# Half of chunk 1's first layer between the parts of chunk 0's second layer, with later joins

## The chip, the cores and the metric

One core of a Trainium2 chip runs the whole kernel. The metric is the device time of one execution in microseconds. Executions of one kernel agree within about 0.3%, and what is argued about here is 0.1% to 0.5%, so every comparison below is of several fast executions of a kernel with those of the kernel before on the same chip, with a 95% interval. Engines: TensorE (PE), its weight loads (PEld), VectorE (DVE), ScalarE (ACT), GpSimd (POOL) and SyncE (SP). The granted clock is the share of TensorE's full clock that its throttle lets through, as the trace records it.

## The reference

```python
def _attn_ref(q, k, v, beta):           # 4 x 8 heads, 768 tokens, head size 48
    k_n = k / (norm(k) + 1e-06)
    for t in range(S):
        y[t] = q[t] @ state
        v_old = state.T @ k_n[t]
        state = state + beta[t] * outer(k_n[t], v[t] - v_old)
def _moe_ref(x, w_in, w_out):           # x is y as 3072 x 384; w_in 384 x 2048
    h = x @ w_in
    return (0.5 * h * (1 + erf(h / sqrt(2)))) @ w_out
```

Inputs and outputs are fp32. What arrives as weights must be decoded on the chip first, on DVE with one step per part on ACT.

## The kernel before

The sequence is cut into 12 chunks of 64 tokens. In each chunk the recurrence becomes small matrix products and a triangular solve. DVE eliminates row by row for two chunks at a time (a group), in blocks of 32. "Joins" then put the blocks together: level 0 (`psJ<-XM,G`) goes back to DVE for a product into XM, level 1 (`psJ<-Zf,XM`) to ACT for a copy into Zf. The chain of a chunk then goes through small products: queries (psG, masked on DVE into P), state products (psK), the solve (psU, copied into U), and from U the output x and the new state (both psY); x is turned (psX) into xT, the feed-forward's input. The feed-forward layer follows: first layer (psH, with a Gelu on ACT), second layer (psO). A scheduler decides the instruction order from a plan of times in which one unit is one chunk's feed-forward. The parts that the change touches (cuts are marked `...`):

```python
def back(x):                       # group g, in eliminate_steps; x = 0, 1, 2
    ...                            # DVE transposes: XM, then twice Zf
    if x == 2:
        for cc in range(2):
            for p in range(2):     # four parts of Zf are cleared
                if g == cc == p == 0: nc.scalar.mul(part, low[...], 0.0)
                else: nc.gpsimd.memset(part, 0.0)

def fc1(c, f):                     # one of 16 first-layer steps
    psH = ps.tile([128, NA * 128], F32, tag="mlp", name="psH")
    for m in range(NM): nc.tensor.matmul(psH, ...)
    nc.scalar.activation(G[:, f, :], psH, ACT.Gelu)

def ffn_steps(c):
    ones = [(1.3, fc1, c, f) for f in range(NF)]
    ...
    twos = [(2.7, fc2, tiles[c, a], f, f + 4) for a in range(NA) for f in range(0, NF, 4)]
    if c == 0: twos.sort(key=lambda s: s[3])
    return ones + twos
...                                # start-up by hand, then the plan
back2[0](*back2[1:])
for a in range(NA): join(0, (a,), 1)
...
plan = [at(c + 1, c + 2, ffn_steps(c)) for c in range(NC)]
plan += [..., at(2.58, 2.74, join_steps(1)), at(2.72, 2.98, state_steps(2)), ...]
```

Of the kernel before, what the change touches and what calls it, by code (L numbers as in the profile page):

```python
# [8 lines left out]
F32 = mybir.dt.float32  # L9
# [7 lines left out]
def kernel(  # L17
# [29 lines left out]
    B, H, S, D = q.shape  # L47
# [235 lines left out]
    def sum_of_squares(u, h):  # L283

        if "both" not in ns:
            n23 = wk.tile([128, 2 * NA, H], F32, tag="n0", name="n0", bufs=1)
            ns[2], ns[3] = n23[:, 0:NA], n23[:, NA:]
            ns["both"] = n23
        if h == 0:
            u.ksq = wk.tile([128, H, D], F32, tag="ksq", name="ksq")  # L290
        nc.scalar.activation(u.ksq[:, h], u.Kn[:, h, 0:D], ACT.Square,
                             accum_out=ns[u.c][:, u.a, h:h + 1])
# [96 lines left out]
    def queries(us):  # L389
        c = us[0].c  # L390
        psP = products(us, 1)
        if c not in Ps:
            Ps[c] = (su if c == 1 else wk).tile([128, NA * H, C], F32, tag=f"P{c == 1}", name="P",
                                                bufs=1)
        for u in us:
            u.P = Ps[c][:, u.a * H:(u.a + 1) * H]
        dst = heads(Ps[c][:, us[0].a * H:(us[-1].a + 1) * H])
        if c < 2:
            nc.scalar.copy(dst, psP)
        else:  # L400
            both = mask.unsqueeze(1).to_broadcast([128, len(us) * H, C])
            nc.vector.tensor_tensor(dst, psP, heads(both), op=ALU.mult)  # L402
# [19 lines left out]
    def eliminate_steps(g):  # L422
        steps = []

        def scales():
            gt = wk.tile([128, HB], F32, tag="gt", name="gt", bufs=1)
            gl = XMs[g] = wk.tile([128, NU, HB], F32, tag="XM", name="XM", bufs=1)
            nc.vector.transpose(gt, gms[g].rearrange("q t h -> q (t h)"))
            nc.gpsimd.tensor_tensor(gl, low, gt.unsqueeze(2).to_broadcast([128, HB, HB]),
                                    op=ALU.mult)  # L430

        def flip():
            Nus[g] = wk.tile([128, HB, HB], F32, tag="Nu", name="Nu", bufs=1)
            nc.vector.transpose(Nus[g], Ds[g].rearrange("q u n -> q n u"))
            nc.vector.tensor_tensor(Nus[g], Nus[g], XMs[g], op=ALU.mult)

        def eliminate(j):
            nu = Nus[g]
            n = HB - 1 - j
            tmp = wk.tile([128, HB * HB // 4], F32, tag="tmp", name="tmp")  # L440
            tmp = tmp[:, 0:n * j].rearrange("q (i c) -> q i c", i=n)
            nc.vector.tensor_tensor(tmp, nu[:, j + 1:, j:j + 1].to_broadcast([128, n, j]),  # L442
                                    nu[:, j:j + 1, 0:j].to_broadcast([128, n, j]), op=ALU.mult)
            nc.vector.tensor_tensor(nu[:, j + 1:, 0:j], nu[:, j + 1:, 0:j], tmp, op=ALU.add)  # L444

        def diagonal():
            flat = Nus[g].rearrange("q i c -> q (i c)")
            nc.vector.memset(flat[:, 0:HB * HB:HB + 1], 1.0)

        def back(x):  # L450
            nu = Nus[g]
            if x == 0:
                nc.vector.transpose(XMs[g].rearrange("q u c -> q c u"),
                                    nu.rearrange("q i c -> q c i"))
            else:
                cols = slice(HB, C) if x == 1 else slice(0, HB)
                nc.vector.transpose(Zf[g % 2][:, :, cols].rearrange("q u i -> q i u"), nu)  # L457
            if x == 2:
                for cc in range(2):
                    for p in range(2):  # L460
                        part = Zf[g % 2][p * C + HB:(p + 1) * C,
                                         cc * NU // 2:(cc + 1) * NU // 2, 0:HB]
                        if g == cc == p == 0:
                            nc.scalar.mul(part, low[0:HB, 0:HB // 2], 0.0)
                        else:
                            nc.gpsimd.memset(part, 0.0)  # L466

        steps = [(0.3, scales), (3.0, flip)]
        steps += [(0.7, eliminate, j) for j in range(1, HB - 1)]
        steps += [(0.1, diagonal)]  # L470
        steps += [(1.9, back, x) for x in range(3)]
        return steps

    def join(g, ts, level, copy=nc.scalar.copy):

# [190 lines left out]


    FH = NF // 2
    DH = DM // 2
    B11, B12 = w_out_sb[:, 0:FH, 0:DH], w_out_sb[:, 0:FH, DH:]  # L670
    B21, B22 = w_out_sb[:, FH:, 0:DH], w_out_sb[:, FH:, DH:]
    T = {}

    def fc1(c, f):
        psH = ps.tile([128, NA * 128], F32, tag="mlp", name="psH")
        for m in range(NM):
            nc.tensor.matmul(psH, lhsT=w_in_sb[:, f // 2, m, f % 2 * 128:(f % 2 + 1) * 128],  # L677
                             rhs=xTs[c][:, m, :], start=(m == 0), stop=(m == NM - 1))
        nc.scalar.activation(G[:, f, :], psH, ACT.Gelu)  # L679
# [112 lines left out]
    def ffn_steps(c):  # L792
        ones = [(1.3, fc1, c, f) for f in range(NF)]
        if c > 1:
            return [(1.3, first_layer, c, f) for f in range(NF)] + [
                (2.6, second_layer, c, n) for n in (1, 5, 2, 6, 4, 7, 3)]
        twos = [(2.7, fc2, tiles[c, a], f, f + 4) for a in range(NA) for f in range(0, NF, 4)]
        if c == 0:
            twos.sort(key=lambda s: s[3])
        return ones + twos  # L800

    def at(first, last, steps):

# [10 lines left out]
    def signs(c0, c1):  # L814
        psB = sq("psB", c1 - c0, B * H)
        for c in range(c0, c1):
            nc.tensor.transpose(psB[:, c - c0, :], bt[:, c].rearrange("n p t -> n (p t)"),
                                ident[0:B * H, 0:B * H])
        for p in range(2):
            src = psB[HALF[p]].rearrange("q c (a p h) -> q c a p h", p=2, h=H)[:, :, :, p, :]  # L820
            nc.scalar.mul(beta_m[HALF[p], c0:c1], src, -1.0)
# [19 lines left out]
    signs(0, 2)  # L841
    diagonals(first[3])
    root(n0)
    scales_, flip_, *rows, back0, back1, back2 = [s_[1:] for s_ in eliminate_steps(0)]
    factors(gms[0], beta_m[:, 0:2].rearrange("q c a h -> q (c a) h"), n0)
    scales_[0]()
    flip_[0]()
# [1 line left out]
    for u in first:  # L849
        grams([u])  # L850
    signs(2, NC)
    for u in first:
        transposed(u, (1,))
        queries([u])
    for a in range(NA):
        fetch_in(tiles[2, a].Qp[:, :, 0:D], q, tiles[2, a])
# [4 lines left out]
    for n in range(n_in, n_in + len(slots)):  # L861
        fetch(n)
    load_v(1)
    third = [tiles[2, a] for a in range(NA)]
    for u in third:
        transposed(u, (0,))
    grams(third)
    for u in third:
        transposed(u, (1,))
# [14 lines left out]
    back2[0](*back2[1:])  # L884
    for a in range(NA):
        join(0, (a,), 1)
    for u in first[NA:]:
        scale_v(u)
    begin(0)
# [27 lines left out]
    def late():  # L917
# [3 lines left out]
        for a in range(NA):  # L921
# [3 lines left out]
            for c in range(5, NC, 2):  # L925
                tiles[c, a].Kb = Kb

    plan = [at(c + 1, c + 2, ffn_steps(c)) for c in range(NC)]
    plan += [at(0.985, 1.26, decode_steps(3, n_in)), at(1.26, 1.65, decode_steps(n_in, NW)), at(1.66, 1.67, [(1.0, late)])]
    plan += [at(0.98, 0.985, [(1.0, load, 3)]),  # L930
             at(1.02, 1.1, [(1.0, join, 0, range(NA, 2 * NA), level) for level in range(2)]),
]
    sums = [(1.0, sum_of_squares, tiles[c, a], h) for c in (2, 3) for a in range(NA) for h in range(H)]
    plan += [at(1.08, 1.5, sums), at(1.51, 1.511, [(1.0, prep, c) for c in (2, 3)]), at(1.65, 1.655, [(1.0, finish_both)]), at(2.97, 2.971, [(1.0, finish, 4)]), at(2.675, 2.676, [(1.0, queries, third)]),
             at(1.12, 1.6, state_steps(1)),
             at(1.75, 2.45, eliminate_steps(1)),
             at(2.58, 2.74, join_steps(1)), at(2.72, 2.98, state_steps(2)),
             at(2.67, 2.671, [(1.0, prep, 4)]), at(2.8, 2.9, [(1.0, grams, [tiles[4, a] for a in range(NA)])])]
    plan += [at(0.995, 1.0, [(1.0, load_v, 2)]), at(2.98, 2.981, [(1.0, sums_of_w)]), at(3.1, 3.11, [(1.0, last_sum_of_w)])]
    plan += [at(c - 0.4, c - 0.3, v_steps(c)) for c in range(4, NC)]  # L940
    plan += [at(2.08, 2.44, [(1.0, scale_head, tiles[c, a], h)
# [2 lines left out]
    for c in range(4, NC):  # L944
        us = [tiles[c, a] for a in range(NA)]
        t = {4: 1.8, 5: 2.1}.get(c, c - 2.9)
        plan += [at(t, t + 0.01, [(1.0, load_blocks, c, "Kb", k)])]
        t = 3.2 if c == 4 else c - (1.3 if c % 2 == 0 else 0.9)
        plan += [at(t, t + 0.01, [(1.0, load_blocks, c, "Qb", q)])]
        t = c - (2.1 if c % 2 == 0 else 2.6) if c > 5 else {4: 2.1, 5: 2.69}[c]  # L950
        plan += [at(t, t + 0.01, [(1.0, load_k, c, "Kn")])]
        plan += [at(c - 0.4, c - 0.39, [(1.0, load_k, c, "Kp")])]
        t = {4: 2.73, 5: 2.95}.get(c, c - (1.97 if c % 2 == 0 else 2.36))
        plan += [at(t, t + 0.01, [(1.0, turned_k, u) for u in us])]
        t = c + (0.05 if c % 2 == 0 else -0.34)
        plan += [at(t, t + 0.01, [(1.0, turned_q, u) for u in us])]
# [56 lines left out]
```

## Time and profile before

| | |
|---|---|
| time | 671.02 us median of 3 runs (670.69 to 671.75) |
| profiled execution | span 670.1 us, a fast one but slower than the three timed (671.82 us of device time) |
| busy | PE 96%, DVE 67%, ACT 34%, POOL 12% |
| start-up, to about 84 us | DVE full, PE 50% to 90% |
| from 178.55 us, chunk 2's first layer | PE without gaps, 101 us per two chunks |

The page's row of the granted TensorE clock (tenths of full speed, 40 slices of 16.75 us):

```profile
PEclk8576999999999999999999999999999999999999
```

The first four slices, the start-up, have less than the full clock. The other lines of before stand in the prediction.

### The profile page before, as it was taken

What the parts mean: (1) busy time and instruction counts of PE and PEld (TensorE: products, weight loads), DVE (VectorE), ACT (ScalarE), POOL (GpSimd) and SP (SyncE); (2) the same over time, 40 slices, a digit from 0 to 9 for tenths busy, and PEclk for the clock granted to TensorE, in tenths of its full rate; (3) what the DMA queues carried; (4) which work ended last, traced back from release to release, by engine and by line L of the source; (5) the groups of instructions that cost most, each with busy time, mean ns of one, the idle gap of its engine ahead of it and who ended that gap; (6) DMA issues with size and microseconds to landing.
All of it is one profiled execution on the core that took longest, in us unless ns stands there. A gap on an engine that the chain in (4) does not pass through costs nothing.

```text
span 670.1 us, 21705 instructions
## 1 busy us (share of the span) xinstructions
PE 640.3 (96%) x9542; PEld 559.4 (83%) x9542; DVE 452.3 (67%) x921; ACT 228.6 (34%) x605; POOL 82.1 (12%) x82
## 2 busy tenths in 40 slices
PE   5767998999999999999999999999999999999997
PEld 4656775866689989989989989989989989989997
DVE  6999999994689846489846479846479844324021
ACT  3357754714342143142143142143142133122220
POOL 4051300103111021111021111021111010000000
PEclk8576999999999999999999999999999999999999
DMA  9785655203431232511332511211401210100101
GB/s 130 174 253 167 121 172 135 48 0 66 81 51 32 53 53 44 82 31 30 55 49 49 84 29 26 53 21 30 68 3 24 55 20 3 24 2 2 24 1 25
DMA packets 158431, 39.76 MB, mean 59 GB/s; under 512 B 150016, under 2 KB 153216, under 8 KB 158336
## 3 DMA queue, kind: packets, MB, share of 16 engines
q1 hardware_dynamic: 152464, 33.40, 26.3%
q10 hardware_dynamic: 5872, 4.97, 3.2%
q8 instruction: 75, 1.23, 0.8%
q14 instruction: 20, 0.16, 0.1%
HBM read 33.62 MB, written 4.72 MB: 57 GB/s over the span
## 4 chain that ended last, share of the span: by engine, by line
PE 82%; DVE 10%; ACT 3%; issue 2%; DMA 2%; SPq 1%; DVEq 0%; ACTq 0%
PE psH L677 36%; PE psX L715 12%; PE psY L715 12%; PE psZ L715 4%; PE psJ L517 3%; PE psK L572 3%; PE psG L367 3%; PE psO L690 2%; PE psU L597 2%; DVE Nu L444 2%; DVE tmp L442 2%; PE psY L615 1%; DVE w_e L235 1%; DVE w_out_sb L236 1%; PE psY L624 1%
## 5 line engine op out<-in xcount | busy, mean ns | idle before, releaser
L677 PE MATMUL psH<-xT,w_in_sb 128*128 128x256 f32 x1152 | 261.5, 383 | 2.3 <-ACT G L679 2.3
L677 PEld LDWEIGHTS psH<-xT,w_in_sb 128*128 128x128 f32 x1152 | 215.6, 190 | 33.7 <-ACT G L679 3.9
L679 ACT ACTIVATE G<-psH 128x256 f32<-128x256 f32 x192 | 73.3, 382 | 180.4 <-PE psH L677 168.3
L444 DVE TENSOR_TENSOR Nu<-Nu,tmp 128x30 f32<-128x30 f32 (+9 forms) x180 | 61.8, 343 | 6.2
L442 DVE TENSOR_TENSOR tmp<-Nu 128x30 f32<-128x30 f32 (+9 forms) x180 | 61.6, 342 | 5.1
L715 PE MATMUL psX<-w_out_sb,G 128*128 128x192 f32 x320 | 56.2, 329 | 0.0
L715 PE MATMUL psY<-w_out_sb,G 128*128 128x192 f32 x304 | 54.1, 329 | 0.6
L715 PEld LDWEIGHTS psX<-w_out_sb,G 128*128 128x128 f32 x320 | 52.2, 190 | 0.7
L715 PEld LDWEIGHTS psY<-w_out_sb,G 128*128 128x128 f32 x304 | 49.1, 190 | 2.1 <-DVE u L761 1.8
L690 PE MATMUL psO<-w_out_sb,G 128*128 128x384 f32 x128 | 45.1, 495 | 1.6 <-DVE w_out_sb L236 1.6
L660 ACT COPY xT<-psX 128x384 f32<-128x384 f32 x24 | 11.3, 476 | 102.9 <-PE psX L659 102.8
L306 POOL TENSOR_TENSOR n<-n,half 128x16 f32<-128x16 f32 x10 | 29.4, 2938 | 87.9 <-DVE n L281 66.9
L690 PEld LDWEIGHTS psO<-w_out_sb,G 128*128 128x128 f32 x128 | 23.1, 190 | 16.9 <-DVE w_out_sb L236 4.0
L603 ACT COPY U<-psU 64x192 f32<-64x192 f32 x96 | 30.0, 313 | 19.5 <-PE psU L597 18.3
L402 DVE TENSOR_TENSOR P<-psG,mask 128x1024 f32<-128x1024 f32 x10 | 12.2, 1224 | 35.6 <-PE psG L367 35.6
L580 DVE TENSOR_TENSOR W<-psK,V 128x384 f32<-128x384 f32 x22 | 12.1, 552 | 29.1 <-ACT y L579 29.0
L466 POOL MEMSET Zf<- 32x512 f32 x23 | 12.4, 541 | 154.5 <-DVE Zf L457 153.6
L724 DVE TENSOR_TENSOR S<-G 128x512 f32<-128x512 f32 x20 | 13.7, 687 | 25.8 <-ACT G L679 25.7
L332 POOL TENSOR_TENSOR V<-V,n 128x384 f32<-128x384 f32 x18 | 17.1, 958 | 106.1 <-DMA V<-in_v_dram 67.6
L638 DVE TENSOR_TENSOR x<-psY,y 64x192 f32<-64x192 f32 x80 | 28.3, 354 | 0.9
L715 PE MATMUL psY<-T,G 128*128 128x192 f32 x160 | 28.2, 329 | 0.0
L715 PE MATMUL psX<-T,G 128*128 128x192 f32 x160 | 28.1, 329 | 0.0
(138 smaller groups left out, 866.9 us busy)
## 6 DMA issues: line engine op xcount, KB each, us to landing
Kp<-in_k_dram SPq DMA_DIRECT2D x76, 96.0 KB, 3.6
w_out_sb<-in_moe_w_in_dram SPq DMA_DIRECT2D x24, 256.0 KB, 4.2
V<-in_v_dram SPq DMA_DIRECT2D x48, 96.0 KB, 2.9
out_dram<-o_sb ACTq DMA_DIRECT2D x46, 96.0 KB, 2.2
w_raw<-in_moe_w_out_dram SPq DMA_DIRECT2D x10, 384.0 KB, 5.4
Zf<-in_moe_w_out_dram SPq DMA_DIRECT2D x6, 384.0 KB, 5.1
Qp<-in_q_dram SPq DMA_DIRECT2D x64, 32.0 KB, 2.2
Qp<-in_q_dram SPq DMA_DIRECT2D x16, 96.0 KB, 4.3
```

What stands on the lines that cost most here:

```text
L306: nc.gpsimd.tensor_tensor(flat, flat, half, op=ALU.pow)
L367: nc.tensor.matmul(psG[HALF[p], r, i * NP + j, :], lhsT=u.Kt[rows, p, j, :], rhs=(u.Qt if x else u.Kt)[rows, p, j, :], start=True, stop=True)
L442: nc.vector.tensor_tensor(tmp, nu[:, j + 1:, j:j + 1].to_broadcast([128, n, j]), nu[:, j:j + 1, 0:j].to_broadcast([128, n, j]), op=ALU.mult)
L444: nc.vector.tensor_tensor(nu[:, j + 1:, 0:j], nu[:, j + 1:, 0:j], tmp, op=ALU.add)
L517: nc.tensor.matmul(psJ[to, i, :], lhsT=(xm if level else off)[rows, u, :], rhs=zf[rows, u, HB:C] if level else xm[rows, u, :], start=True, ...
L572: nc.tensor.matmul(u.psK[to, x, r, j, :], lhsT=(u.Qt if x else u.Kt)[rows, p, j, :], rhs=St[rows, u.a, p, j, :], start=True, stop=True)
L603: copy(pairs(u.U[HALF[p]], s), u.psU[HALF[p ^ s], p])
L638: nc.vector.tensor_tensor(dst, src, pairs(u.y[HALF[p ^ s]], s), op=ALU.add)
L677: nc.tensor.matmul(psH, lhsT=w_in_sb[:, f // 2, m, f % 2 * 128:(f % 2 + 1) * 128], rhs=xTs[c][:, m, :], start=(m == 0), stop=(m == NM - 1))
L679: nc.scalar.activation(G[:, f, :], psH, ACT.Gelu)
L690: nc.tensor.matmul(u.psO, lhsT=G[:, f, u.a * 128:(u.a + 1) * 128], rhs=w_out_sb[:, f, :], start=(f == 0), stop=(f == NF - 1))
L715: nc.tensor.matmul(ps_, lhsT=lhs[:, f, :], rhs=rhs[:, f, :], start=first and f == 0, stop=f == FH - 1, skip_group_check=not first)
```

## The change

The intent is to fill TensorE's waits for decoded output weights in chunk 0's second layer with half of chunk 1's first layer (C), to start the decode earlier by taking a clear out of the way of ACT's copies (A), to move 16 squares of chunk 2's norm into start-up (B), and to place the joins and what follows later in the plan (D). The lines are shortened, those of the plan to the times that change; the tile of the moved sums also gets another buffer.

```diff
-            if x == 2:
+            if x == 2 and g > 0:
+                clear(g)
+        def clear(g):
                 for cc in range(2): ...
-        return steps
+        return steps + [(0.0, clear, 0)] if g == 0 else steps      # A
...
+    EARLY = 8
     def fc1(c, f):
-        psH = ps.tile([128, NA * 128], F32, tag="mlp", name="psH")
+        if c == 1 and f < EARLY: psH = dn("psH")[:, 0, 0:NA * 128]
+        else: psH = ps.tile([128, NA * 128], F32, tag="mlp", name="psH")
...
         if c == 0:
             twos.sort(key=lambda s: s[3])
-        return ones + twos
+            more_ = [(1.3, fc1, 1, f) for f in range(EARLY)]       # C
+            return ones + twos[:-2*NA] + more_[:4] + twos[-2*NA:-NA] + more_[4:] + twos[-NA:]
+        return ones[EARLY:] + twos
...
     for u in first:
         transposed(u, (1,))
+        for i in range(4 if u.t > 1 else 0): sum_of_squares(*next(some))   # B
         queries([u])
...                                # after chunk 2's first transposes:
+    for left in some: sum_of_squares(*left)                        # B
...
     for a in range(NA):
         join(0, (a,), 1)
+    clear_[0](*clear_[1:])                                         # A
...
-    plan = [at(c + 1, c + 2, ffn_steps(c)) for c in range(NC)]
+    plan = [at(c + 1 + 0.25 * (c == 1), c + 2 + 0.25 * (c == 0), ffn_steps(c)) ...]
-    sums for c in (2, 3); at(1.08, 1.5, sums); queries at 2.675
+    sums for c = 3;       at(1.2, 1.5, sums);  queries at 2.725
-    at(2.58, 2.74, join_steps(1)), at(2.72, 2.98, state_steps(2)), ...
+    at(2.64, 2.77, join_steps(1)), at(2.76, 2.985, state_steps(2)), ...    # D
     (chunk 4's and 5's loads and transposes 0.005 to 0.05 later)
```

More of the change, by code (lines that the diff above doesn't have):

```diff
@@ L285, in sum_of_squares @@
         if "both" not in ns:
-            n23 = wk.tile([128, 2 * NA, H], F32, tag="n0", name="n0", bufs=1)
+            n23 = wk.tile([128, 2 * NA, H], F32, tag="root", name="n23", bufs=1)
             ns[2], ns[3] = n23[:, 0:NA], n23[:, NA:]
@@ L674, in fc1 @@
     def fc1(c, f):
-        psH = ps.tile([128, NA * 128], F32, tag="mlp", name="psH")
+        if c == 1 and f < EARLY:
+            psH = dn("psH")[:, 0, 0:NA * 128]
+        else:
+            psH = ps.tile([128, NA * 128], F32, tag="mlp", name="psH")
         for m in range(NM):
@@ L799, in ffn_steps @@
             twos.sort(key=lambda s: s[3])
-        return ones + twos
+            more_ = [(1.3, fc1, 1, f) for f in range(EARLY)]
+            return ones + twos[:-2 * NA] + more_[:4] + twos[-2 * NA:-NA] + more_[4:] + twos[-NA:]
+        return ones[EARLY:] + twos
     def at(first, last, steps):
@@ L843 @@
     root(n0)
-    scales_, flip_, *rows, back0, back1, back2 = [s_[1:] for s_ in eliminate_steps(0)]
+    scales_, flip_, *rows, back0, back1, back2, clear_ = [s_[1:] for s_ in eliminate_steps(0)]
     factors(gms[0], beta_m[:, 0:2].rearrange("q c a h -> q (c a) h"), n0)
@@ L851 @@
     signs(2, NC)
+    third = [tiles[2, a] for a in range(NA)]
+    some = iter([(u, h) for u in third for h in range(H)])
     for u in first:
         transposed(u, (1,))
+        for i in range(4 if u.t > 1 else 0):
+            sum_of_squares(*next(some))
         queries([u])
@@ L863 @@
     load_v(1)
-    third = [tiles[2, a] for a in range(NA)]
     for u in third:
         transposed(u, (0,))
+    for left in some:
+        sum_of_squares(*left)
     grams(third)
@@ L926, in late @@
                 tiles[c, a].Kb = Kb
-    plan = [at(c + 1, c + 2, ffn_steps(c)) for c in range(NC)]
+    plan = [at(c + 1 + 0.25 * (c == 1), c + 2 + 0.25 * (c == 0), ffn_steps(c)) for c in range(NC)]
     plan += [at(0.985, 1.26, decode_steps(3, n_in)), at(1.26, 1.65, decode_steps(n_in, NW)), at(1.66, 1.67, [(1.0, late)])]
@@ L932 @@
 ]
-    sums = [(1.0, sum_of_squares, tiles[c, a], h) for c in (2, 3) for a in range(NA) for h in range(H)]
-    plan += [at(1.08, 1.5, sums), at(1.51, 1.511, [(1.0, prep, c) for c in (2, 3)]), at(1.65, 1.655, [(1.0, finish_both)]), at(2.97, 2.971, [(1.0, finish, 4)]), at(2.675, 2.676, [(1.0, queries, third)]),
+    sums = [(1.0, sum_of_squares, tiles[3, a], h) for a in range(NA) for h in range(H)]
+    plan += [at(1.2, 1.5, sums), at(1.51, 1.511, [(1.0, prep, c) for c in (2, 3)]), at(1.65, 1.655, [(1.0, finish_both)]), at(2.97, 2.971, [(1.0, finish, 4)]), at(2.725, 2.726, [(1.0, queries, third)]),
              at(1.12, 1.6, state_steps(1)),
              at(1.75, 2.45, eliminate_steps(1)),
-             at(2.58, 2.74, join_steps(1)), at(2.72, 2.98, state_steps(2)),
-             at(2.67, 2.671, [(1.0, prep, 4)]), at(2.8, 2.9, [(1.0, grams, [tiles[4, a] for a in range(NA)])])]
+             at(2.64, 2.77, join_steps(1)), at(2.76, 2.985, state_steps(2)),
+             at(2.72, 2.721, [(1.0, prep, 4)]), at(2.8, 2.9, [(1.0, grams, [tiles[4, a] for a in range(NA)])])]
     plan += [at(0.995, 1.0, [(1.0, load_v, 2)]), at(2.98, 2.981, [(1.0, sums_of_w)]), at(3.1, 3.11, [(1.0, last_sum_of_w)])]
@@ L949 @@
         plan += [at(t, t + 0.01, [(1.0, load_blocks, c, "Qb", q)])]
-        t = c - (2.1 if c % 2 == 0 else 2.6) if c > 5 else {4: 2.1, 5: 2.69}[c]
+        t = c - (2.1 if c % 2 == 0 else 2.6) if c > 5 else {4: 2.1, 5: 2.74}[c]
         plan += [at(t, t + 0.01, [(1.0, load_k, c, "Kn")])]
         plan += [at(c - 0.4, c - 0.39, [(1.0, load_k, c, "Kp")])]
-        t = {4: 2.73, 5: 2.95}.get(c, c - (1.97 if c % 2 == 0 else 2.36))
+        t = {4: 2.76, 5: 2.955}.get(c, c - (1.97 if c % 2 == 0 else 2.36))
         plan += [at(t, t + 0.01, [(1.0, turned_k, u) for u in us])]
```

## The prediction

> **What bounds the kernel now.** I first read the page of the kernel before: TensorE (PE) is busy 96% of a span of 670.1 us, VectorE (DVE) 67%. The row of forty slices, 16.75 us each, says where the missing 4% lies.
>
> ```profile
> PE   5767998999999999999999999999999999999997
> DVE  6999999994689846489846479846479844324021
> ```
>
> The first five slices are start-up, bound by DVE. Slices six to seven (84 to 117 us) hold 9 and 8 for PE and 9 for DVE. From there PE is full. So I asked for busy time by stage; the columns are start:end, length, then busy us (and instructions) of PE, weight loads, DVE, ScalarE (ACT), GpSimd, then the granted clock, DMA share, GB/s.
>
> ```profile
> 93.50:120.10 26.60, 24.79 (x90) 14.53 (x89) 26.05 (x38) 11.53 (x24) 1.46 (x1) 1.00 0.58 151
> 120.10:141.10 21.00, 20.99 (x98) 18.08 (x97) 19.02 (x53) 12.20 (x45) 0.46 (x1) 1.00 0.21 36
> 141.10:178.50 37.40, 35.27 (x793) 23.09 (x791) 23.29 (x44) 11.97 (x27) 8.60 (x7) 1.00 0.31 53
> 178.50:279.60 101.10, 100.75 (x1570) 91.34 (x1571) 76.53 (x154) 31.74 (x77) 14.78 (x13) 1.00 0.33 51
> ```
>
> Row one is chunk 0's second layer: PE idles 26.60 - 24.79 = 1.8 us, and DVE is the full engine (26.05 of 26.60), because it is decoding the output weights that this layer multiplies by. Row two is chunk 1's first layer: no idle. Row three is chunk 1's second layer with the joins and state of chunk 2: 2.1 us idle. Row four is the repeating part (101 us per two chunks): 0.35 us idle. Everything after 178.5 us is PE work without gaps, which no reordering shortens. The idle that this change can reach is in rows one and three and in the start-up.
>
> The timeline of PE over row one (start, length, engine, line, operation, output and inputs, count, in brackets the idle before and what ended it):
>
> ```profile
> 106.06 4.04 PE L690 MATMUL psO<-w_out_sb,G 128*128 128x384 f32 x12
> 110.26 2.85 PE L690 MATMUL psO<-w_out_sb,G 128*128 128x384 f32 x8 [0.17 <-DVE w_out_sb L236]
> 114.05 2.85 PE L690 MATMUL psO<-w_out_sb,G 128*128 128x384 f32 x8 [0.94 <-DVE w_out_sb L236]
> 117.38 2.85 PE L690 MATMUL psO<-w_out_sb,G 128*128 128x384 f32 x8 [0.47 <-DVE w_out_sb L236]
> 120.06 21.16 PE L677 MATMUL psH<-xT,w_in_sb 128*128 128x256 f32 x96
> ```
>
> Each group of 8 waits for one decoded weight part, which DVE delivers every 3.3 to 3.8 us, while the 8 matmuls need 2.6 us. Behind them stand 96 matmuls of chunk 1's first layer that need no such weight: its input is complete at about 106.9 us, after ACT's copies of it.
>
> The start of the decode is held by another chain, read from the timelines of ACT, PE and DVE:
>
> ```profile
> 47.68 0.63 ACT L464 ACTIVATE Zf<-low 32x512 f32<-32x512 f32 x1 [3.95 <-DVE Zf L457]
> 48.32 1.51 ACT L499 COPY Zf<-psJ 32x256 f32<-32x256 f32 x4
> 49.16 1.96 PE L597 MATMUL psU<-W,Zf 64*64 64x48 f32 x64 [2.32 <-ACT Zf L499]
> 59.60 0.96 DVE L235 SCALAR_TENSOR_TENSOR w_e<-w_out_sb,w_e 128x768 uint32<-128x768 uint32 x1 [0.91 <-ACT w_e L223]
> ```
>
> ACT clears a quarter of Zf only after DVE has written it, and its four copies of the join, whose matmuls end at 46.8, queue behind that clear. This runs through psU, U, x and xT to an exponent step on ACT at 58.6, for which DVE idles 0.91 us. From 59.6 to 117.3 us DVE has one more wait, 0.47 us.
>
> **What the Trainium skill says.** "Perfetto Trace Analysis", Optimization Strategy: where the most contended engine changes over time, interleaving the regimes may help. That is the case here: DVE 98% in row one, PE 100% in row two. "PSUM — Partial Sum Buffer", Engine vs sequencer instructions: ScalarE, VectorE and GpSimd queues are strict FIFO and matmuls start and complete in program order. The trace agrees: at 114.05 PE stands still although runnable first-layer matmuls are next; and ACT's copies wait 3.95 us behind a clear that they do not need. The same page, Specifications: 8 banks of 512 fp32 values per partition. The kernel uses them all: "dn" 2 x 2 banks, "mlp" 2, the small tag 2. Both "mlp" banks hold chunk 0's two sums, so the early first layer must borrow "dn" tiles. "ScalarE: Activation LUTs", Rules for kernel authors, budgets about 0.3 us plus 0.83 ns per element: 0.51 us for 256; the trace has 0.38 us for a Gelu of 256 columns, so that is what I use.
>
> **The change, part by part.** The instruction orders of the two kernels show identical sequences on DVE and GpSimd; PE and ACT are reordered, SP slightly. No work is added.
>
> A. The clear of group 0 comes after the last join. ACT's four copies can then run as soon as psJ is there: the first two from about 45.6, the last two by 47.4; then the clear, 47.68 to 48.3. The first GpSimd clear, which psU also needs, is done at about 48.4 in either kernel. So psU starts at about 48.5 and finishes near 49.6 instead of 51.1: 1.5 us for the chain PE-ACT. DVE can use only its own wait, 0.91 us: the decode runs 0.9 us earlier from 59.6 on, and all that follows it.
>
> B. The 16 squares of chunk 2 (0.225 us apart on ACT, so 3.6 us) move from 59-67 us to the row steps. Two sets of four (0.9 us) stand in ACT idle gaps of 1.25 us before a P copy, free. The last eight (1.8 us) follow the Kt copy ending at 34.4, and the next copy was due at 35.8: ACT slips 0.4 us. The join's first matmuls wait for DVE until 42.1; the slipped copies free its second buffer at about 42.9, and DVE takes the result only at 43.9. Hidden. In the stage it leaves, Gelu is held by exponent steps, which wait for DVE, so I count no gain.
>
> C. Eight of sixteen first-layer steps of chunk 1 go into the gaps. One step is 6 matmuls, 21.16/16 = 1.3 us; 8 are 10.4 us. Without A: the first half of the second layer and the turn end at 107.4. Four steps to 112.6; 16 matmuls of 0.325 us (5.2) to 117.8, their weights there at 110.2; four steps to 123.0; the last 16 to 128.2, weights there at 117.3. Before, the same work ends at 120.06 + 10.4 = 130.4. Gain 2.2 us, more than the three waits' sum of 1.6 because each restart also loses some tenths of weight load. With A, 3.1 us.
>
> D. Joins and chunk 2's state. PE arrives 3.1 us earlier, DVE's row steps end 0.9 us earlier (145.1 for XM). PE's order now has 24 second-layer matmuls ahead of the first join (16 before), then both groups' first joins together, so that DVE's four XM products run without their wait:
>
> ```profile
> 150.22 0.24 PE L517 MATMUL psJ<-XM,G 32*32 32x32 f32 x2
> 151.06 0.18 PE L517 MATMUL psJ<-Zf,XM 32*32 32x32 f32 x1 [0.59 <-issue]
> 152.34 1.40 DVE L525 TENSOR_TENSOR XM<-psJ,gm 32x512 f32<-32x512 f32 x2 [1.39 <-PE psJ L517]
> ```
>
> Following PE step by step with durations from the trace: first layer done 137.7, 24 matmuls 145.5, joins 147.75, four matmuls 149.05, a wait of about 1.0 for XM (150.05), join 151.2, queries 153.6, join 154.75, state products 159.4, solve 164.2, state update 169.2, chunk 2's first layer at about 173.6 to 174.2 instead of 178.55. That is 4.4 to 4.9 us, of which 1.3 to 1.8 from D. The wait of 2.07 us that ACT shows at 159 behind an output transfer leaves the path of y too, since that transfer is now issued earlier.
>
> Sum: A 0.9 + C 2.2 + D 1.3 (the lower figure) = 4.4. After that the pattern repeats, PE-bound, and keeps the shift: 671.0 - 4.4 = 666.6 us.
>
> **Rivals.** (1) The join wait takes the gain. PE arrives 3.1 us early, DVE 0.9; what is won in C is stood out at 147 to 152. For it: DVE's row steps are packed and unchanged. Against: 8 more matmuls (2.6 us) were placed ahead of the join. If C came to nothing: about 669.5. (2) ACT becomes the bound at 117 to 125. The Kb clears stay in ACT's queue and in the trace waited 4.29 us for the decode to end; behind them V scalings come five to a Gelu: 5 x 0.23 + 0.36 = 1.5 us against PE's 1.3. Against: these four Gelus are needed one at a time, with two buffers. It might cost 0.5 us: 667.1. (3) A's start-up gain is absorbed: if the copies still had to wait for DVE's second Zf write, psU would start at about 49.9 and gain nothing: 667.5. The order's waits show a separate DVE wait on the clear after the copies', which speaks for the free version. (4) The eight squares hold up the join: 0.5 to 1 us, all DVE work shifted: 667.5. (5) DVE, 76% busy after 178.5, cannot keep up with PE's shift in chunk 2's mixes; it starts that stretch after a wait of 7.6 us for PE, so it moves along.
>
> **Range and chances.** All rivals together leave a gain near 1.5; everything going well, D and some of the 1.4 us that PE waits for ACT at 66 us, a gain of 6. Range 664.7 to 669.2, with 666.6 the middle. 2% is 13.4 us; the idle that PE has from 93.5 to 178.5 is only 1.8 + 2.1 us, and the start-up's rest is not touched, so faster by 2% is nearly excluded, and a loss of 2% would need a stall of 13 us.
>
> **What would show it.** Right: psU starts near 48.5; the DVE wait of 0.91 at 59.6 is gone and the last decode ends near 116.4; no wait for w_out_sb after 107 us; PE idle before the second join about 1 us; chunk 2's first layer starts near 174. Wrong: PE stands on DVE XM for over 2 us at about 148; psU still at 49 or later; early Gelus over 2 us late behind Kb or V; or a new wait after 178 us, where I expect the same 101 us per two chunks.

## The result, and the profile after

The changed kernel takes 667.89 us (median of 6 runs, 667.4 to 668.6) beside 670.79 us of the kernel before (6 runs, 670.61 to 671.75). The ratio is 0.9956, 95% interval 0.9943 to 0.9968. Ratios here are the mean time of one kernel's fast runs over that of the other's of the same rounds, so they are not quite the ratio of the medians. The gain is 2.9 us, within 2%, as predicted; 4.4 us had been predicted, and 667.89 lies inside the range. The two profiles differ by 3.8 us (spans 670.1 and 666.3): the profiled execution of before, at 671.82 us, was 1.0 us above its median.

The page of the kernel after, the row of forty slices:

```profile
PE   6777999999999999999999999999999999999997
```

The digits 9, 8 of slices six and seven are now 9, 9. The same four stretches by stage (columns as in the prediction):

```profile
93.50:120.10 26.60, 26.32 (x109) 18.45 (x108) 25.83 (x39) 13.35 (x34) 1.92 (x1) 1.00 0.60 152
120.10:141.10 21.00, 21.00 (x86) 16.06 (x85) 19.21 (x53) 10.20 (x38) 0.00 (x0) 1.00 0.22 35
141.10:178.50 37.40, 36.00 (x800) 25.57 (x799) 25.82 (x46) 12.57 (x28) 9.49 (x8) 1.00 0.36 64
178.50:279.60 101.10, 100.80 (x1574) 91.52 (x1574) 74.61 (x156) 31.85 (x77) 13.52 (x11) 1.00 0.33 52
```

PE's idle time in row one falls from 1.81 to 0.28 us, with DVE as full as before; in row three from 2.13 to 1.40. Row four has not changed. The timeline of PE over the part that C fills (in brackets, here and below, the idle time before and what ended it; `issue` means that the profile names nothing):

```profile
106.87 5.34 PE L684 MATMUL psH<-xT,w_in_sb 128*128 128x256 f32 x24
112.05 5.32 PE L697 MATMUL psO<-w_out_sb,G 128*128 128x384 f32 x16
117.21 5.34 PE L684 MATMUL psH<-xT,w_in_sb 128*128 128x256 f32 x24
122.39 5.32 PE L697 MATMUL psO<-w_out_sb,G 128*128 128x384 f32 x16
127.55 10.52 PE L684 MATMUL psH<-xT,w_in_sb 128*128 128x256 f32 x48
```

No row has a bracket: the three waits for w_out_sb are gone. Chunk 1's first layer ends at 137.91 instead of 141.06. The start of the decode, timelines of PE and DVE, and psU's matmuls once more where a later chunk has them:

```profile
48.49 2.03 PE L600 MATMUL psU<-W,Zf 64*64 64x48 f32 x64 [1.57 <-issue]
59.00 0.96 DVE L235 SCALAR_TENSOR_TENSOR w_e<-w_out_sb,w_e 128x768 uint32<-128x768 uint32 x1 [0.32 <-ACT w_e L223]
82.43 1.15 PE L600 MATMUL psU<-W,Zf 64*64 64x48 f32 x64
```

The busy times of the two stretches; the number after POOL's count is the granted clock:

```profile
82.40:83.50 1.10, 1.10 (x65) 1.02 (x64) 1.10 (x2) 0.38 (x1) 0.00 (x0) 1.00 0.49 89
48.50:50.50 2.00, 2.00 (x64) 1.86 (x64) 1.97 (x4) 0.85 (x1) 1.81 (x4) 0.50 0.04 10
```

psU starts 0.67 us earlier, as predicted, but its 64 matmuls need 2.03 us at half the clock, and 0.32 of DVE's 0.91 us wait is left. The joins, PE and DVE:

```profile
145.74 2.21 PE L520 MATMUL psJ<-XM,G 32*32 32x32 f32 x128
147.88 1.56 PE L697 MATMUL psO<-w_out_sb,G 128*128 128x384 f32 x4
150.52 1.20 PE L520 MATMUL psJ<-Zf,XM 32*32 32x32 f32 x64 [1.08 <-issue]
```

Both level-0 joins stand together, and PE waits 1.08 us for the first level-1 join. DVE's four XM products run from 149.03 to 151.85 without a wait; the first two are done near 150.4, just before the join starts. Chunk 2's first layer starts at 174.76 instead of 178.55.

One number per profile then tells almost everything: when chunk 2's first layer starts. What comes after it takes the same time in every profile at the normal pace, read from the PE timelines:

| kernel | psU starts | chunk 2's first layer starts | span | rest |
|---|---|---|---|---|
| before | 49.16 | 178.55 | 670.1 | 491.55 |
| after | 48.49 | 174.76 | 666.3 | 491.54 |
| after, third time | 48.70 | 175.37 | 666.9 | 491.53 |
| after without A | 49.14 | 175.24 | 666.8 | 491.56 |
| after without B | 48.42 | 174.40 | 665.9 | 491.50 |
| A + B + C (no D) | 48.73 | 176.91 | 668.4 | 491.49 |
| A + B only | 48.22 | 176.84 | 668.4 | 491.56 |
| A + B + D (no C) | 49.46 | 176.97 | 668.5 | 491.53 |

The rest is 491.5 us to within 0.04; the four other profiles at this pace, of the runs further down, have 491.52 to 491.56. The first two columns also show that start-up itself scatters: with A, psU starts anywhere from 48.2 to 49.5 (49.7 in the last run below), and that moves all that follows. So single profiles are not compared to better than about 1 us; the timed ratios decide.

### The profile page after: what moved, and what is told of

Same layout as the page of the kernel before. It is cut to its first block, busy times and chain, and to the rows that moved or that the text cites. A ratio compares the mean times of both kernels' runs of the same rounds, so it can differ in the third digit from the quotient of the medians.

```text
span 666.3 us, 21708 instructions
## 1 busy us (share of the span) xinstructions
PE 641.8 (96%) x9542; PEld 562.7 (84%) x9542; DVE 452.1 (68%) x921; ACT 228.9 (34%) x605; POOL 83.6 (13%) x82
## 3 DMA queue, kind: packets, MB, share of 16 engines
q8 instruction: 75, 1.23, 0.8%
## 4 chain that ended last, share of the span: by engine, by line
PE 89%; ACT 4%; DVE 3%; issue 2%; DMA 1%; SPq 0%; ACTq 0%
PE psH L684 36%; PE psX L722 12%; PE psY L722 12%; PE psO L697 5%; PE psG L367 4%; PE psZ L722 4%; PE psK L575 3%; PE psJ L520 3%; PE psU L600 2%; PE psT L346 2%; PE psY L618 2%; PE psY L627 1%; ACT U L606 1%; PE psX L662 1%; DVE w_e L235 1%
## 5 line engine op out<-in xcount | busy, mean ns | idle before, releaser
L606 ACT COPY U<-psU 64x192 f32<-64x192 f32 x96 | 30.0, 313 | 20.5 <-PE psU L600 19.2
```

Of the source, the lines that this page charges most:

```text
L606: copy(pairs(u.U[HALF[p]], s), u.psU[HALF[p ^ s], p])
```

## The experiments

My theory: A is worth 0.5 us because psU runs at half pace, B nothing, and C and D need each other. The rivals stand in the texts below. Ratios are to the kernel before on the same chip, with the 95% interval.

**The changed kernel again.**

> A control: the changed kernel once more, on the chip that the next three run on. Its profile before showed a span 3.8 us shorter than that of the kernel before, its times only 2.9 us. Theory: the difference is the spread of single runs (each kernel's six runs spread over 1.1 us, and the profiled run of the kernel before was its slowest), so the ratio comes out at 0.9950 to 0.9962 again, and this second profile differs from the first by up to 1 us, in the start-up (before 60 us). Rival: the profiles are right and the times are pulled by something after 180 us; then this profile shows a stage after 180 us that is longer than 101 us per two chunks.

The median is 667.98 us, ratio 0.9955 (0.9942 to 0.9968), as expected of the times. The profile fell into an execution of 1629.2 us, the first of its batch of runs. Its costliest group of instructions, the first layer's matmuls (busy us, mean ns), and the same group of the first profile of after:

```profile
L684 PE MATMUL psH<-xT,w_in_sb 128*128 128x256 f32 x1152 | 694.6, 832 | 0.0
```

```profile
L684 PE MATMUL psH<-xT,w_in_sb 128*128 128x256 f32 x1152 | 261.4, 383 | 2.4 <-ACT G L686 2.3
```

Only matmuls and their weight loads are slower; a Gelu has 384 ns on average in one and 382 in the other. This execution explains nothing about the change and is left out.

**Without A.**

```diff
+    clear_[0](*clear_[1:])
     for a in range(NA):
         join(0, (a,), 1)
-    clear_[0](*clear_[1:])
```

> The changed kernel with the clear of Zf put back ahead of the last join's copies; only ACT's order of these five instructions differs. My prediction gave this part 0.9 us. Theory now, from the trace: psU does start 0.7 us earlier, but its 64 matmuls take 2.0 us, as long as before, because TensorE runs at half pace there, so the part is worth 0.5 to 0.6 us: time = changed kernel + 0.5 us (range 0.3 to 0.8), DVE's first wait at 59 us back to 0.9, last decode step ends 0.5 us later. Rival (the prediction's size): + 0.9 us. Rival (start-up absorbed later, where PE waits for XM): + 0.0 to 0.2 us.

668.53 us, ratio 0.9963 (0.9951 to 0.9975), 0.5 us above the changed kernel of the same batch, and in the trace both old waits are back:

```profile
49.14 2.04 PE L600 MATMUL psU<-W,Zf 64*64 64x48 f32 x64 [2.32 <-ACT Zf L502]
59.65 0.96 DVE L235 SCALAR_TENSOR_TENSOR w_e<-w_out_sb,w_e 128x768 uint32<-128x768 uint32 x1 [0.91 <-ACT w_e L223]
```

The waits show what A does without doubt: 0.91 against 0.32 us, so 0.59 us of DVE; the wait is 0.32 to 0.34 us in all eight profiles that have A (the runs with dummies and with later exponents apart, which change more in the start-up). The time agrees with that, though the two intervals overlap.

**Without B.** The squares go back to their old place (`at(1.08, 1.5, sums)` for chunks 2 and 3, none in the row steps).

> The changed kernel with the 16 squares of chunk 2 back among the first layer's Gelus. Theory: worth nothing, 0.0 +- 0.3 us, since Gelu there is held by the exponent steps that wait for DVE; the start-up may even gain 0.1 us because ACT's copies of group 1 come 0.4 to 1.2 us earlier and the join's second half (PE idle 0.20 at 43.7) no longer waits. Rival: the squares delay Gelu and so the first layer; then PE's waits for G between 60 and 93 us grow from 2.3 us and the time by 0.5 us or more.

668.23 us, ratio 0.9958 (0.9946 to 0.9970) beside 0.9955: B is worth nothing that can be measured (each interval is 0.8 us to either side).

**Without D.** A, B and C stay; the joins, chunk 2's state and the loads get their old times.

```diff
-    at(2.64, 2.77, join_steps(1)), at(2.76, 2.985, state_steps(2)), queries 2.725
+    at(2.58, 2.74, join_steps(1)), at(2.72, 2.98, state_steps(2)), queries 2.675
```

> The changed kernel with all times of the joins, states and loads of chunk 2 to 5 as in the kernel before: 8 second-layer matmuls ahead of the first join in place of 12, the two groups' joins mixed again. Theory: PE comes to the first join 2.6 us too early, at about 143 us, waits for XM until 145.4, and waits again at the mixed join; it loses 2.0 to 3.5 us, so the time is that of the kernel before within 1 us (changed kernel + 2 to + 3): the later joins are what lets the filled gap be kept. Rival: PE makes the time up because the total of PE work ahead of chunk 2's first layer is the same and DVE's chain is short enough; then + 0.0 to 0.7 us.

670.5 us, ratio 0.9996 (0.9984 to 1.0009): the gain is gone. PE's timeline shows where:

```profile
138.14 5.32 PE L697 MATMUL psO<-w_out_sb,G 128*128 128x384 f32 x16
145.75 1.20 PE L520 MATMUL psJ<-XM,G 32*32 32x32 f32 x64 [2.29 <-DVE XM L453]
146.88 4.54 PE L697 MATMUL psO<-w_out_sb,G 128*128 128x384 f32 x8
```

PE arrives early at the first join and waits 2.29 us for XM, which DVE's row steps deliver at 145.6. Then comes something that I had not thought of: the 8 matmuls after it take 4.54 us, where the same 8 take 2.85. Four stretches of this trace give the reason:

```profile
146.00:147.00 1.00, 1.00 (x61) 0.96 (x55) 1.00 (x1) 0.00 (x0) 0.00 (x0) 1.00 0.00 0
147.00:148.00 1.00, 1.00 (x2) 0.58 (x3) 1.00 (x2) 0.00 (x0) 0.00 (x0) 0.53 0.00 0
149.00:150.00 1.00, 1.00 (x3) 0.50 (x2) 0.95 (x3) 0.00 (x0) 0.72 (x2) 0.50 0.00 0
151.00:152.00 1.00, 1.00 (x77) 0.65 (x78) 0.00 (x0) 0.00 (x0) 0.46 (x1) 1.00 0.05 16
```

After the wait the clock is halved from about 147 to 150.5, and the 8 matmuls take 4.54 - 2.85 = 1.7 us more. This aftermath does not reach the end, though. From the join's start to chunk 2's first layer it is 31.16 us here and 31.31 in the kernel with A and B only (further down), at full clock: that one has two waits of 0.63 and 0.68 us in this stretch, which PE, coming later, does not meet here. What takes the gain is the wait of 2.29 us. That the clock falls in every execution is not shown; one execution was profiled.

**The kernel before against itself.**

> The kernel before against itself: a control of the method and a second profile of before, whose first profile fell in its slowest run (671.82 us). Theory: ratio 1.000 +- 0.001; in the profile psU (line 597) starts near 49.2, DVE's wait at 59.6 near 0.9 us and chunk 2's first layer near 178.5, all within 0.3 us of the first profile. Rival: the profile of before was an unlucky one and these places move by 0.5 us or more, so the 3.8 us between the two profiles overstates the gain.

671.21 us, ratio 0.9994 (0.9981 to 1.0008), so the method is sound. The profile was again lost to a slow first execution (1288.88 us), this time of the kernel before. Whether the places in the first profile of before repeat stays unanswered.

**A and B only.** `EARLY = 0` and all times of the plan as before.

> The changed kernel with C and D undone: no early first layer of chunk 1 and the old times of the joins; A (the clear behind the copies) and B (the squares moved) stay. Theory: A is worth 0.5, B nothing, so 670.8 - 0.5 = 670.3 us, ratio 0.9993. With the run without later joins (670.5, ratio 0.9996) this says that C alone, without D, brings nothing, and C with D 2.4 us. Rival (additive parts, as the prediction's sum has them: A 0.9, C 2.2, D 1.3): 669.9 here and a clear 0.5 to 1 us difference from the run without later joins. Second rival: the first-layer steps in the gaps do more harm than good without D, then this kernel is faster than the run without later joins by 0.3 us or more.

670.81 us, ratio 0.9999 (0.9985 to 1.0013). The theory's 0.9993 and the rival's 0.9987 both lie within the interval, so A's value cannot be settled by this time. What it does settle: C added to this without D gives 0.9996, that is nothing, against the additive sum, which would have it 2.2 us faster. Its PE waits 0.96 and 0.47 us for w_out_sb at 113.27 and 116.59, as before the change.

PE's order from there to chunk 2's first layer is that of the kernel before, yet the way from the end of chunk 1's first layer is 36.56 us (140.28 to 176.84) where before has 37.49. The two lines that issue the output transfer on ACT, before and here:

```profile
159.00 2.07 ACTq L684 DMA_DIRECT2D out_dram<-o_sb  x2
158.31 1.16 ACTq L691 DMA_DIRECT2D out_dram<-o_sb  x2
```

In the profile of before ACT is held 0.91 us longer, its next copies (of y) come that much later, and PE ends up waiting 0.61 us for xT at 177.44, a wait that this run lacks. The chain that ends at chunk 2's first layer, followed back by the profiler's view of it, runs through that issue in before and not here. All eleven other profiles at the normal pace have 1.12 to 1.69 us for this issue. So about 0.9 us of what the profile of before showed was peculiar to that execution, as far as one profile of it can tell.

**Dummy matmuls in the start-up.** 15 small matmuls fill PE's idle places from 40 to 58 us.

```diff
+    def warm(n):
+        psW = sq("psW", 128)
+        for i in range(n):
+            nc.tensor.matmul(psW, lhsT=ident, rhs=ident, start=True, stop=True)
```

> The changed kernel plus 15 small dummy matmuls (128x128 identity) in TensorE's idle places between 40 and 58 us. It tests why psU took 2.03 us at 48.5 and 1.15 us at 82.4 with the same 64 matmuls. Theory (TensorE runs at half pace there because it had been mostly idle before): psU takes 1.2 to 1.5 us, U's copies start 0.5 to 0.8 us earlier, DVE's wait of 0.32 us at 59.0 goes, and the time falls by 0.3 us to 667.6 (0.6 at most, since DVE has only waits of 0.32 and 0.64 us to give before 117 us). Rival (the 64 products of psU wait for their operands one by one, or the pace does not answer to dummy work): psU stays near 2.0 us, and the time stays or rises by up to 0.3 us. Inconclusive if psU comes out between 1.6 and 1.9.

670.27 us, ratio 0.9980 (0.9968 to 0.9993): slower than the changed kernel by more than either theory allowed. PE's timeline and the clock of two of its stretches:

```profile
48.56 1.96 PE L600 MATMUL psU<-W,Zf 64*64 64x48 f32 x64
58.30 1.15 PE L627 MATMUL psY<-U,Kp 64*64 64x48 f32 x64
```

```profile
46.00:47.00 1.00, 1.00 (x29) 0.96 (x22) 1.00 (x1) 0.83 (x3) 0.33 (x1) 1.00 0.48 66
48.00:49.00 1.00, 0.96 (x18) 0.73 (x21) 0.96 (x2) 0.97 (x2) 0.95 (x2) 0.50 0.07 14
```

With dummies the clock was full up to 47.9 us (0.50 from 40 us on in the profile of after), and psY's 64 matmuls at 58 us took 1.15 instead of 1.96. But PE was only 22% busy from 47 to 48, the clock fell at 48, and psU ran at half pace all the same. And the dummies stood in the way: the second psX starts at 57.60 instead of 56.72, and DVE's wait at 59 grew from 0.32 to 1.24 us. So the half pace is the granted clock, and the expectation for psU failed. DVE comes out of that wait 0.75 us later than in the first profile of after and meets another at 78.22, of 0.59 us for a DMA; chunk 1's first layer then ends 1.21 us later (139.12) and chunk 2's starts 0.98 later (175.74). A later decode thus goes through to the end, though two waits share in it here. The profiled execution, 669.02 us, is one of the two fast ones of the five; the other three took 670.27 to 670.67, and why is open.

**Exponent steps later.** The order of steps in the decode, `start_ = begin + exponents` split so that `exponents` follows `signed`.

> The changed kernel with one thing altered that neither version has: in the decoding of the weights the exponent step on ScalarE is emitted behind the DVE step of the part before it instead of ahead of it, so that a Gelu of chunk 0's first layer no longer queues behind an exponent step that is still waiting for DVE. TensorE's waits for G at 65.7 (1.41 us), 72.2 (0.51) and 86.7 (0.38) would shrink. Theory (DVE, not TensorE, sets the time up to about 117 us and again at the second join near 150): TensorE's gain of up to 2 us there is stood out at the second join, whose wait grows from 1.08 to 2 us or more, and the time stays within 0.5 us of the changed kernel, or gets worse if DVE now waits for exponents. Rival (TensorE's idle time is lost wherever it stands): 1 to 2 us faster than the changed kernel, near 666.3, which would beat both.

668.8 us, ratio 0.9962 (0.9949 to 0.9974). The edit did not do what it was for: PE's wait for G at 65.9 is still 1.41 us, DVE's wait at 59 is 0.51. It therefore tells nothing between the theories, only that this order is no better.

**Without C.** The missing corner: A, B and D, `EARLY = 0`.

> The changed kernel without C: no early first layer, with A, B and the later joins (D). It is the missing corner beside A+B (ratio 0.9999), A+B+C (0.9996) and all four (0.9955). Theory (the second join waits for VectorE's XM, so an earlier TensorE pays only if there is other work to put before that join; and work before the join pays only if TensorE arrives early): without C TensorE reaches the joins 2.6 us later, the 8 matmuls more before the first join are work that the old order did after it at no loss, so D alone saves only the two waits of about 0.6 us that the mixed joins had: 669.6 to 670.6 us, ratio 0.998 to 1.000. Rival (D is worth by itself what its absence cost, 2.5 us): 668.2 us, ratio 0.996 or less.

669.62 us, ratio 0.9976 (0.9963 to 0.9988). The theory's range (0.998 to 1.000) is missed by a little, with the interval reaching into it, and the rival's (0.996 or less) clearly. With the other corners:

| A and B, and | without D | with D |
|---|---|---|
| without C | 0.9999 | 0.9976 |
| with C | 0.9996 | 0.9955 |

In microseconds of 671: C alone 0.2, D alone 1.5, both 3.0. C is worth 1.4 when D is there, and D 2.75 when C is. Each corner is uncertain by about 0.9 us, so the interaction of 1.2 us, uncertain by an estimated 1.7 (four such corners, taken as independent), is not shown by the times.

The traces can tell more if the scatter of start-up is taken out: DVE's work up to its wait near 59 us does not depend on the change, so I count from the moment at which that wait begins (58.69 us before, 58.68 after).

| kernel | to the end of chunk 1's first layer | from there to chunk 2's first layer |
|---|---|---|
| before | 82.37 | 37.49 |
| A + B | 81.88 | 36.56 |
| A + B + C | 79.22 | 38.77 |
| A + B + D | 81.87 | 35.44 |
| after, first and third | 79.23, 79.27 | 36.85, 37.21 |
| after without A | 79.84 | 36.66 |

The first column is nearly free of scatter. In it A is worth 0.5 to 0.6 us and C 2.5 to 2.7, with or without D. In the second column C takes 2.2 us back without D (the wait of 2.29) and 1.4 to 1.8 with D. There the level-1 join, which has no wait when C is absent, has one of about 1.1:

```profile
152.99 1.20 PE L520 MATMUL psJ<-Zf,XM 32*32 32x32 f32 x64
```

So C nets 0.4 to 0.5 us without D and 0.8 to 1.2 with it, and D 1.1 without C and 1.6 to 1.9 with it: an interaction of 0.4 to 0.8 us, smaller than the times suggest, from one profile of each corner and two of after.

**The second joins moved apart.** An attempt to beat both kernels: the four joins get times of their own, the level-1 joins behind four more second-layer matmuls, the queries after them.

```diff
-    at(2.64, 2.77, join_steps(1))
+    level 0 at 2.662 and 2.663, level 1 at 2.72 and 2.76; queries 2.765; state from 2.785
```

> An attempt to beat both: the changed kernel with the second joins moved behind four more second-layer matmuls (1.3 us), both second joins together, the queries after them. Theory: TensorE's remaining wait of 1.08 us at 150.5 goes, since VectorE's first two XM products are ready at 150.4; chunk 2's first layer starts at 173.7 to 174.3 instead of 174.8, and the time falls by 0.5 to 1.0 us to 667.2. Rival (ScalarE becomes the one waited for: its copies of the second join now queue behind an output's copy and its DMA issue, 1.2 us, and behind a norm step; the queries need the buffer that those copies free): TensorE waits 1 us or more at the queries or at the state products instead, and the time stays at 667.9 or rises by up to 1 us.

668.82 us, ratio 0.9966 (0.9953 to 0.9978). The changed kernel took 668.59 on the same chip, and the rival came true: the wait left the join and stood at the queries, whose buffer ACT's copies free late.

```profile
156.07 1.16 PE L367 MATMUL psG<-Qt,Kt 48*64 48x64 f32 x64 [1.19 <-ACT Zf L532]
```

**The changed kernel a third time.**

> The changed kernel once more, for a second profile in the fast state (the second profile asked for before fell into an execution in which TensorE ran at a third of its pace) and for times beside the other two on the same chip. Theory: 667.9 us, ratio 0.9955 +- 0.0013; psU starts near 48.5 and takes 2.0 us; VectorE's wait near 59.0 is 0.3; the wait before the second join 1.1; chunk 2's first layer at 174.8, each within 0.3 us of the first profile. Rival: these places move by 0.5 us or more between two executions of the same kernel, and the first profile's differences of that size say nothing.

668.59 us, ratio 0.9955 (0.9942 to 0.9969), the same ratio for the third time. In the profile psU starts at 48.70 and takes 2.03 us, DVE's wait is 0.33, PE's wait at the joins 1.11: within 0.3 us. Chunk 2's first layer starts at 175.37, 0.6 later than in the first profile. Of that 0.2 is start-up and 0.3 lies at the state products, which take 2.58 us up to the next matmuls, 2.27 in the first profile and 2.01 without C. So at that place the claim of 0.3 failed.

**The joins apart, mended.** The last two parts of chunk 1's two tiles change places, so that the output's copy and its DMA issue come behind the join's copies, and the queries come after eight second-layer matmuls.

```diff
+        if c == 1:
+            twos[3], twos[4] = twos[4], twos[3]
```

> The attempt to beat both once more, with what stopped the first one mended: the second joins behind four more second-layer matmuls as there, but chunk 1's first tile gets its last four matmuls after the second joins instead of before them, so its output's copy and DMA issue come behind ScalarE's copies of the join; the queries come after eight second-layer matmuls, when those copies have freed their buffer. Theory: both waits are gone (1.08 to 1.11 us before the second join in the changed kernel, 1.19 us before the queries in the first attempt); the state products start at about 157.0 to 157.4 instead of 158.1 to 158.4, chunk 2's first layer 0.8 to 1.1 us earlier than in the changed kernel for the same start of psU, and the time is 667.0 to 667.4 (ratio 0.994 to 0.9945). Rival (a wait further down, before the products of U or at chunk 2's transposes, which stand behind ScalarE's copies of U, takes it back): the state products start earlier but chunk 2's first layer does not, and the time stays at 667.9 to 668.6, ratio 0.9955 to 0.9965. The first kernel of a call has twice had a very slow first execution here; then only the times tell, not the profile.

671.16 us, ratio 0.9992 (0.9978 to 1.0006): it lost everything, more than the rival had said. PE's timeline:

```profile
151.91 2.53 PE L520 MATMUL psJ<-Zf,XM 32*32 32x32 f32 x128
159.66 0.68 PE L575 MATMUL psK<-St,Kt 48*64 48x48 f32 x32 [0.43 <-DVE P L402]
162.10 0.45 PE L575 MATMUL psK<-St,Qt 48*64 48x48 f32 x3 [1.30 <-issue]
162.48 4.20 PE L697 MATMUL psO<-w_out_sb,G 128*128 128x384 f32 x8
```

The join's wait is gone, but the state products now wait 0.43 us for DVE's P, which follows the later queries, and 1.30 us more for nothing that the profile names. Then the clock is at 0.50 from 161.8 to 165.2, and 8 matmuls take 4.20 us instead of 2.85. Sum: 0.43 + 1.30 + 1.35 = 3.1 us lost for 1.1 won. Here the slow matmuls do go through: from their start to chunk 2's first layer it is 15.70 us, 14.35 in the first profile of after. What PE stood on for the 1.30 us is open. The five times fall into two groups, 669.93 and 669.95, and 671.16 to 671.54; the profile is of the slower, so the fall of the clock need not be in all five. No version here beats the changed kernel.

## Why the prediction was right or wrong

**The bound.** Right. The rest from chunk 2's first layer on is 491.5 us in every profile at the normal pace, so only what happens before it counts.

**A, predicted 0.9 us: this step failed.** psU did start at 48.5, but "finishes near 49.6 instead of 51.1" did not come: it finished at 50.5. I had taken the 1.96 us of psU before for a wait plus 1.1 us of work. It is all work, at a granted clock of 0.50; the same 64 matmuls take 1.15 us at 82.43, at 1.00. In its place the runs have 0.59 us less DVE wait and 0.5 to 0.6 us at the end of chunk 1's first layer. The times (0.5 us when A is taken out of the changed kernel, 0.1 for A and B alone) agree, but each is uncertain by 0.9. One reading beside it was loose too: the 3.95 us are ACT's idle time before the clear, not the copies' wait. The matmuls of their join ran from 44.88 to 46.83, so the last copies stood about 1.5 us behind the clear.

**B, predicted 0.** Right: 0.9958 without it, 0.9955 with it. ACT slips more than the 0.4 us counted (1.23 us at the copies near 42, from 41.38 to 42.61), and it is hidden all the same: the level-1 join starts at 44.88 in both profiles.

**C, predicted 2.2 us.** The place is right: the first layer done at 137.91 for a predicted 137.7, no wait for w_out_sb left. At that place it is worth 2.5 to 2.7 us. That A and C together gave the predicted 3.1 there (3.15 measured) is luck: one term was too large and the other too small.

**D, predicted 1.3 us (the lower figure) for the way from there to chunk 2's first layer.** This term holds the net of D's gain and of what C's lead is stood out for. Between the profiles of before and after it is 0.64 us, and 0.28 with the third profile of after, in place of 1.3 to 1.8 (or 1.0 to 1.6 by the places of the prediction's own walk, 137.7 to 173.6 or 174.2). Two causes are seen. First, the wait that D leaves, predicted as about 1.0, is 1.08 and 1.11, as counted, but the path behind it is longer: from the second-layer matmuls after the last join (155.36) to the end of the state products (160.41) it takes 5.05 us where I had counted 4.65. Second, the 37.49 us of before from which I stepped have about 0.9 us of a long output issue, which the A and B run, with the same order, does not have; against its 36.56 us, C and D together gain nothing on this way. D alone, without C's lead, gains 1.1 there by the traces and 1.5 by the times.

The times give 2.9 us for the predicted 4.4. By the traces A and C come in as a sum, and what is missing is in D's stage and in the profile from which the prediction started. The split by the times alone (A and B 0.1, C and D 3.0) would blame A for 0.8 us, but lies within its uncertainty.

**The rivals.** (1), the join wait takes the gain, is the mechanism of the kernel without D: 2.2 us of C's 2.5 to 2.7 are lost there. With D it is still half true, with 1.4 to 1.8. (2) did not bite: PE has no wait from 106.87 to the joins. (3) came half true, though by psU's pace and not by the copies. (4) and (5) did not occur.

## What to carry to other kernels

Filling a gap makes the engine arrive early at its next meeting with a slower one. Move work to before that meeting in the same change and count both as one term, because here the fill was all but lost without the move. A wait of the bound engine can cost more than its length when the clock falls after it (1.35 us in the last run), so look at the pace of the instructions that follow, and then at whether later waits take it back, as in the kernel without D. Do not step from one profile without asking which of its waits a second one would show; and take a duration for work or for waiting only after comparing it with the same work elsewhere in the trace.

## What the Trainium skill lacked or had wrong

- "TensorE: Matmul & The Clock Gate", Part 1 (the HAM clock gate, its two states), has the clock fall after an idle window of about 3.4 us; its section on psum-queue depth-cycling has frequent short idles do it too, without a length. In these traces less idle time sufficed: in the 3.41 us before the fall PE was idle for 2.1 us in one kernel (of its wait of 2.29) and for 1.44 in another. The page's free-running window does agree with the traces: halved stretches last 3.4, 10.2, 17.1, 20.5 and 23.9 us, which are 1, 3, 5, 6 and 7 times 3.41, and in one profile the clock comes back at 61.72 and falls again at 147.06, 25.0 times 3.41 later.
- No page says what counts as busy when matmuls are small. In the changed kernel PE is busy for 6.63 of the 7 us from 40 to 47, with 192 of its 195 matmuls on 48x64 or 32x32 of the array, and the clock stays at 0.50. The 1.44 us of idle time that came with a fall stood among state products on 48x64 of the array; 1.41 us of idle time before 65.70 in the changed kernel stood among first-layer matmuls on all of it, and the clock stayed at 1.00. That small matmuls count for less is an inference; no run isolates it.
- "TensorE: Matmul & The Clock Gate", "Seeing it yourself", mentions a throttle stuck for over 50 us and doubtful records. Here two whole executions, of either kernel, took 1629 and 1289 us with matmuls at 832 and 680 ns instead of 383 while the recorded granted clock was 1.00 throughout. Both were the first execution of a batch of runs; in two other batches the first was normal.
